# A joint input projection by twenty block products instead of twenty-two

## The chip, the core and the metric

The kernel runs on one core of a Trainium2 chip. A core has five engines that work side by side, each on its own list of instructions, in order: TensorE (PE in the profile, with its weight loads as PEld), VectorE (DVE), ScalarE (ACT), GpSimd (POOL) and SyncE (SP), which here only issues DMAs. They wait for each other through semaphores. TensorE writes to PSUM, a small accumulator memory; VectorE and ScalarE read results out of it. The metric is the time of one execution in microseconds (us) on the device.

## The reference

The program computes two blocks in a row. The first is a linear attention (RWKV-6) with a per-channel decay, for 4 batches, 8 heads, 768 tokens and a head dimension of 48:

```
for t in range(S):
    cur = outer(u * k[t], v[t])
    y[t] = r[t] @ (state + cur)
    state = w[t][:, None] * state + outer(k[t], v[t])
```

Its output, rearranged to 3072 tokens of 384 channels, is x of the second block, a feed-forward layer with 2048 hidden channels:

```
h = x @ w_in                                  # 384 -> 2048
sp = max(h, 0) + log1p(exp(-abs(h)))          # softplus
g = h * erf(sp)
out = g @ w_out                               # 2048 -> 384
```

Everything is in float32.

## The kernel before

The 3072 tokens are worked through in twelve units (`n_steps`, n in the text; the last two are n−2 and n−1) of 256 tokens (128 tokens of two batches). For each unit the attention makes `xT`: three tiles of 128 channels by 256 tokens, channels on the partitions. The feed-forward of a unit follows one to three steps later and is spread in small pieces between the attention's instructions of later units, so that TensorE always has something to do. There is no automatic scheduler: the order is written out by hand (`tc.manual_schedule`), and every engine gets its instructions in the order in which the Python code issues them. `run_late` reads a string of letters and issues one piece for each. The letters that matter here:

- `P` and `Q`: a piece of the output projection (`project_fast`, L1245), of the unit three or two steps back. It is eight matmuls, one of seven block products by which a unit's output is made (a 2x2x2 scheme with seven products in place of eight). Its sums lie in two PSUM tiles `m`, of a pool with two buffers. DVE adds the last products to `o` (L1265, L1270), and SP sends `o` out.
- `S`: `blend`, four DVE instructions (L1222 to L1228) that make the left factors of the seven products from the unit's hidden values, once all of these are there.
- `J`: a piece of the joint input projection (`hidden_of_two`), `T`: its preparation (`join_tokens`), `w`: one instruction of `join_weights`.
- `u`, `v`, `z` (`activate_pair`): softplus of one 128x512 chunk of hidden values on ACT, erf of it on ACT, and the product with the hidden values on DVE. ACT loads a table whenever it changes between softplus and erf.

The input projection of most units (`hidden`, L1123) takes 48 matmuls a unit: 16 groups of 128 hidden channels by three groups of 128 input channels. For the last two units, which come when no attention is left to interleave with, it is done jointly. Two units' tokens, the two halves of the hidden channels (`NG` = 2, eight groups each) and the input channels make a block product, which `hidden_of_two` computes by a scheme with 22 block products for 24. It runs over four pairs of channel groups; in each pair it makes seven pieces `J`, 22 matmuls of 128x256 in all. The sums lie in PSUM in three places: `m0` in the tile `y` and `low` and `high` in the two `pp` tiles; each of the three takes half of both banks of its tile. ACT or DVE reads every finished sum into the hidden values h11, h12, h21, h22 (L1342 to L1365), and a chunk that is complete goes to the list `chunks`, from which `u` takes it.

The weight sums for the joint projection (L1297) and the token differences (L1310) are made by DVE before it starts. In the last attention step (`LATE[n_steps - 1]`) and the lines behind the loop over the steps (at the end of the kernel function) their places among the other pieces are written out.

[...]

Of the kernel before, what the change touches and what calls it, by code (L numbers as in the profile page):

```python
# [11 lines left out]
FP32 = mybir.dt.float32  # L12
# [40 lines left out]
def rights(ap, half):  # L53

    names = "abcdefg"[: len(ap.shape) - 1]
    spread = " ".join(names)
    return ap.rearrange(f"{spread} (n two h) -> {spread} n two h", two=2, h=half)[
        (slice(None),) * len(names) + (slice(None), 1)
    ]


@with_exitstack
def kernel(
# [1004 lines left out]
    later, chunks, started = [], [], []  # L1068
# [136 lines left out]
    def blend(of, *parts):  # L1205

        if of not in blends:
            if of < n_steps - 2:
                tiles = [room[:, n] for n in (1, 2, 3)]
            elif of == n_steps - 1:  # L1210
                tiles = [half_room("words", [P, 2, DM, 2])[:, : FG * C] for _ in range(3)]
            else:
                two = att.tile([P, 2, JP, C], FP32, name="rk1", bufs=1)
                one = ins.tile([P, JP, C], FP32, name="w")
                tiles = [x.rearrange("p n t -> p (n t)") for x in (two[:, 0], two[:, 1], one[:])]
            s1, s2, s4 = (x.rearrange("p (f t) -> p f t", t=C) for x in tiles)
            blends[of] = s1, s2, quarter(of, "21"), s4
        s1, s2, s3, s4 = blends[of]
        a = {what: quarter(of, what) if what not in lanes else lanes[what] for what in ("11", "12", "22")}
        for part in parts or (1, 2, 4, 3):  # L1220
            if part == 1:
                nc.vector.tensor_add(s1, s3, a["22"])  # L1222
            elif part == 2:
                nc.vector.tensor_sub(s2, s1, a["11"])
            elif part == 3:
                nc.vector.tensor_sub(s3, a["11"], s3)
            else:
                nc.vector.tensor_sub(s4, a["12"], s2)  # L1228
# [52 lines left out]
    def third(g, kk):  # L1281

        return w_in_sb[:, g * FG : (g + 1) * FG, kk * P : (kk + 1) * P]

    def join_weights():

        s1, s2, s4 = (
            half_room("words", [P, 2, DM, 2])[:, : FG * P].rearrange("p (f m) -> p f m", m=P)
            for _ in range(3)
        )  # L1290
        a11, a12, a21, a22 = (third(g, kk) for g in range(NG) for kk in range(2))
        turns["joint weights"] = s1, s2, a21, s4
        for out_, a, op, b in (
            (s1, a21, ALU.add, a22), (s2, s1, ALU.subtract, a11),
            (s4, a12, ALU.subtract, s2), (a21, a11, ALU.subtract, a21),
        ):
            nc.vector.tensor_tensor(out=out_, in0=a, in1=b, op=op)  # L1297
            yield

    def join_tokens():  # L1300

        made = ins.tile([P, 2, JP, C], FP32, name="in")
        made = made[:].rearrange("p x n t -> p (x n t)").rearrange("p (i t) -> p i t", t=UNIT)
        t1, t2, t3, t4, less = (made[:, i] for i in range(5))
        one, two = ([xTs[of][:, kk, :] for kk in range(KT)] for of in (n_steps - 2, n_steps - 1))
        for out_, a, b in (
            (t1, two[0], one[0]), (t2, two[1], t1), (t4, one[1], t2), (less, one[2], two[2]),
            (t3, two[1], two[0]),
        ):
            nc.vector.tensor_sub(out_, a, b)  # L1310
        turns["joint tokens"] = one, two, t1, t2, t3, t4, less

    def hidden_of_two():
# [3 lines left out]
        h12 = room[:, 2:4].rearrange("p i n -> p (i n)").rearrange("p (f t) -> p f t", t=UNIT)  # L1317
        h22 = ins.tile([P, 2, JP, C], FP32, name="in")
        h22 = h22[:].rearrange("p x n t -> p (x n t)").rearrange("p (f t) -> p f t", t=UNIT)
        gated[one].extend((h11, h21))  # L1320
        gated[two].extend((h12, h22))
        m0 = y[:, :, 0].rearrange("p e j t -> p e (j t)")
        low, high = (products([P, NE, 2, UNIT], n)[:, :, 0] for n in range(2))

        s1, s2, s3, s4 = turns["joint weights"]
        x, z, t1, t2, t3, t4, less = turns["joint tokens"]
        a11, a12, up, _, a22, down = (third(g, kk) for g in range(NG) for kk in range(KT))

        def add_up(to, start, *factors):

            for k, (a, b) in enumerate(factors):
                for e in range(NE):
                    nc.tensor.matmul(  # L1333
                        to[:, e], lhsT=a[:, 2 * i + e], rhs=b,
                        start=start and not k, stop=True, skip_group_check=True,
                    )

        pairs = FG // 2
        for i in range(pairs):
            f = slice(2 * i, 2 * i + 2)  # L1340
            add_up(m0, True, (a11, x[0]))
            nc.scalar.copy(h11[:, f], m0)  # L1342
            yield
            add_up(low, True, (a12, x[1]), (up, x[2]))
            nc.vector.tensor_add(h11[:, f], h11[:, f], low)
            chunks.append(h11[:, f])
            yield
            add_up(high, True, (s1, t1))
            nc.scalar.copy(h22[:, f], high)
            yield  # L1350
            add_up(m0, False, (s2, t2))
            nc.vector.tensor_copy(h12[:, f], m0)
            yield
            add_up(low, True, (a22, t4), (down, less))
            nc.scalar.copy(h21[:, f], low)
            yield
            add_up(m0, False, (s3, t3), (down, z[2]))
            nc.vector.tensor_add(h21[:, f], h21[:, f], m0)
            nc.vector.tensor_add(h22[:, f], h22[:, f], m0)
            chunks.append(h21[:, f])  # L1360
            if i < pairs - 2:
                chunks.append(h22[:, f])
            yield
            add_up(high, False, (s4, z[1]), (up, z[2]))
            nc.vector.tensor_add(h12[:, f], h12[:, f], high)  # L1365
            if i < pairs - 2:
                chunks.append(h12[:, f])
            elif i == pairs - 1:
                chunks.extend(h[:, 2 * i - 2 : 2 * i + 2] for h in (h12, h22))
            yield  # L1370
# [3 lines left out]
    def activate_pair(what):  # L1374

        if what == "u":
            h = chunks.pop(0)
# [45 lines left out]
    def in_order(s, k):  # L1423
# [15 lines left out]
            "s P", "m w", "ey P m s P P ep P", "m P P", "", "", ""  # L1439
# [7 lines left out]
    def run_late(s, tokens, following=None):  # L1447

        for what in tokens.split():
# [16 lines left out]
            elif what == "T":  # L1466
                join_tokens()
                turns["joint"] = hidden_of_two()
            elif what == "f":
# [26 lines left out]
    joining = join_weights()  # L1496
# [15 lines left out]
    with tc.manual_schedule(  # L1512
# [81 lines left out]
        run_late(s - 1, "S Q w w w")  # L1594
        from_own(s - 1, ready[s - 1][0], 0)
        through_state(s - 1, xTs[s - 1])
        run_late(s, "P P P P T")
        run_late(s, "J J J J J u J u u J")
        run_late(s, "J u v J J v J z z J v v J z u u u J z")
        run_late(s, "J u v J J v J z z J v v J z u u J z")  # L1600
        run_late(s, "J J u v J J z v J z v J z u v J z P P S s ey")
        run_late(s + 1, "P P m s ep P P m P P P S")
# [97 lines left out]
```

## Time and profile before

Three runs took 576.76, 577.13 and 577.54 us. The profiled execution has a span of 575.4 us from its first to its last instruction; its own time outside the span is not recorded, and the median of the runs lies 1.7 us above the span.

| stretch (us from the start) | length | PE busy | DVE busy | ACT busy | granted TensorE clock |
|---|---|---|---|---|---|
| last attention step up to the joint projection, 439.82 to 492.74 | 52.92 | 52.92 | 29.05 | 27.31 | 1.00 |
| joint projection, 492.74 to 530.72 | 37.98 | 37.98 | 19.05 | 28.08 | 1.00 |
| output projection of the last two units and the end, 530.72 to 575.40 | 44.68 | 41.60 | 16.66 | 13.89 | 1.00 |

How to read it: a row is a stretch of the span, and each number the time in which the engine had an instruction at work. An engine's instructions overlap a little at their ends, so the time from one start to the next is somewhat shorter than the duration of one. A bracket behind an instruction in the timelines, such as [2.83 <-PE y L1333], says that the engine was idle for 2.83 us before it, and which instruction ended that. A float32 matmul leaves two records in the trace, so a count of 4 is two matmuls. The last store to memory is issued at 572.74 and lands at about 574.35.

### The profile page before, as it was taken

The numbers are of one execution on the slowest core, as the hardware profiler recorded it, in microseconds if no ns is written. First come the engines' busy times: TensorE is split into PE (matmuls) and PEld (weight loads), VectorE is DVE, ScalarE is ACT, GpSimd is POOL, SyncE is SP. The second block draws the span as 40 slices with busy tenths as digits, with TensorE's granted clock in tenths as the row PEclk, the third lists the DMA queues.
The fourth block names the chain that finished last, engine by engine and source line by source line (L and its number), as shares of the span: only waits on it lengthen the run. The fifth ranks groups of instructions, "written<-read, shape, count | busy, mean of one in ns | idle before, by whom it ended". The sixth has DMA issues, their size and how long they took to land.

```text
span 575.4 us, 16716 instructions
## 1 busy us (share of the span) xinstructions
PE 568.1 (99%) x7336; PEld 503.9 (88%) x7336; DVE 442.7 (77%) x475; ACT 358.0 (62%) x488; POOL 244.7 (43%) x265
## 2 busy tenths in 40 slices
PE   8999999999999999999999999999999999999997
PEld 6688777678998998998998998998898899988997
DVE  7785887999899998798699699599599527255640
ACT  3668777645458858748747756766766661388700
POOL 4567381632885883393384284185173000000000
PEclk9999999999999999999999999999999999999999
DMA  7595662350435325155145145234232201000000
GB/s 263 192 348 214 240 205 68 161 164 3 147 84 168 109 66 171 21 176 166 18 159 167 32 145 172 40 121 162 39 120 74 48 8 37 1 1 2 27 28 27
DMA packets 54081, 63.24 MB, mean 110 GB/s; under 512 B 35160, under 2 KB 40568, under 8 KB 52984
## 3 DMA queue, kind: packets, MB, share of 16 engines
q1 hardware_dynamic: 53624, 61.98, 34.0%
q8 instruction: 57, 0.93, 0.7%
q10 hardware_dynamic: 384, 0.20, 0.1%
q14 instruction: 16, 0.13, 0.1%
HBM read 52.39 MB, written 8.69 MB: 106 GB/s over the span
## 4 chain that ended last, share of the span: by engine, by line
PE 93%; DVE 4%; ACT 2%; issue 1%; POOL 0%; DVEq 0%; ACTq 0%; POOLq 0%
PE m L1245 34%; PE m L1123 33%; PE pp L641 5%; PE pp L1333 4%; PE m L1155 4%; PE y L1333 2%; PE y L673 2%; PE y L699 2%; PE pp L748 2%; PE m L951 1%; DVE in L334 1%; PE pp L960 1%; PE pp L1033 1%; DVE h L1088 1%; ACT rest L267 0%
## 5 line engine op out<-in xcount | busy, mean ns | idle before, releaser
L1123 PE MATMUL m<-xT,w_in_sb 128*128 128x256 f32 x960 | 215.0, 382 | 0.9 <-ACT h L1132 0.7
L1123 PEld LDWEIGHTS m<-xT,w_in_sb 128*128 128x128 f32 x960 | 179.8, 190 | 26.5 <-ACT h L1132 1.4
L334 DVE TENSOR_TENSOR in<-in,tot_sb 128x1024 f32<-128x1024 f32 (+1 forms) x55 | 80.1, 1457 | 12.7 <-PE pp L641 11.4
L1132 ACT COPY h<-m 128x512 f32<-128x512 f32 x80 | 46.1, 580 | 48.5 <-PE m L1123 48.4
L1245 PE MATMUL m<-mixed,h 128*128 128x192 f32 x320 | 56.7, 331 | 0.0
L1245 PE MATMUL m<-w_out_sb,h 128*128 128x192 f32 x320 | 56.2, 329 | 0.0
L1245 PEld LDWEIGHTS m<-mixed,h 128*128 128x128 f32 x320 | 51.8, 190 | 1.0
L1245 PE MATMUL m<-w_out_sb,room 128*128 128x192 f32 x304 | 52.5, 326 | 0.0
L1245 PEld LDWEIGHTS m<-w_out_sb,h 128*128 128x128 f32 x320 | 52.0, 190 | 0.5
L1245 PEld LDWEIGHTS m<-w_out_sb,room 128*128 128x128 f32 x304 | 49.9, 190 | 0.0
L1083 ACT ACT_TABLE_LOAD x30 | 38.5, 1283 | 10.7 <-DVE h L1088 8.5
L463 POOL TENSOR_TENSOR words<-words,own 128x384 f32<-128x384 f32 x21 | 30.1, 1432 | 22.8 <-DVE words L494 13.0
L504 POOL TENSOR_TENSOR words<-words 128x384 f32<-128x384 f32 x28 | 39.7, 1447 | 0.0
L1079 ACT ACT_TABLE_LOAD x30 | 38.5, 1283 | 1.8 <-issue 1.3
L641 PEld LDWEIGHTS pp<-in 48*48 48x48 f32 (+4 forms) x2368 | 30.1, 120 | 10.8 <-issue 3.5
L456 POOL TENSOR_TENSOR own<-rest 128x384 f32<-128x384 f32 x7 | 9.7, 1379 | 61.0 <-ACT o L1251 61.0
L641 PE MATMUL pp<-in 48*48 48x32 f32 (+4 forms) x2368 | 33.9, 206 | 0.2 <-DVE in L334 0.2
L504 POOL TENSOR_TENSOR rk<-words 128x384 f32<-128x384 f32 x28 | 33.4, 1220 | 0.0
L529 DVE TENSOR_REDUCE sums<-rk 128x16 f32<-128x768 f32 (+2 forms) x31 | 31.6, 1020 | 0.0
L408 POOL TENSOR_TENSOR tot_sb<-tot_sb 128x256 f32<-128x256 f32 (+4 forms) x50 | 28.8, 576 | 3.8
L1079 ACT ACTIVATE room<-h 128x1024 f32<-128x1024 f32 x28 | 29.6, 1057 | 0.3
L1245 PE MATMUL m<-mixed,room 128*128 128x192 f32 x160 | 27.7, 327 | 0.0
(206 smaller groups left out, 981.6 us busy)
## 6 DMA issues: line engine op xcount, KB each, us to landing
in<-in_rkw SPq DMA_DIRECT2D x8, 1024.0 KB, 5.2
words<-in_moe_w_in SPq DMA_DIRECT2D x16, 384.0 KB, 5.4
words<-in_moe_w_out SPq DMA_DIRECT2D x16, 384.0 KB, 5.2
words<-in_rk_rows SPq DMA_DIRECT2D x8, 768.0 KB, 6.1
w<-in_rkw SPq DMA_DIRECT2D x11, 512.0 KB
v<-in_v SPq DMA_DIRECT2D x12, 384.0 KB, 5.6
out<-o SPq DMA_DIRECT2D x23, 192.0 KB, 3.0
in<-in_rkw SPq DMA_DIRECT2D x7, 512.0 KB, 5.6
```

The lines of the kernel that those rows point to most:

```text
L334: nc.vector.tensor_mul(halves, halves, view(tots[level - 1], 0, [[1, n], [2, nb], [0, half]]))
L408: nc.gpsimd.tensor_mul(new, pair[:, :, 0], pair[:, :, 1])
L463: engine.tensor_mul(to, to, of[:, :, None, :].to_broadcast([P, NEAR // 2 // half, half, D]))
L504: engine.tensor_mul(to[:, i], r[:, half:], k[:, part * rows + i, None].to_broadcast([P, half, D]),)
L529: nc.vector.tensor_reduce(out=to, in_=of, axis=mybir.AxisListType.X, op=ALU.add)
L641: nc.tensor.matmul(to, lhsT=rk(1, n)[rows(e), s0 : s0 + m], rhs=right, start=True, stop=True,)
L1079: nc.scalar.activation(sp_room, chunks[0], AF.Softplus)
L1083: nc.scalar.activation(at, sp_room, AF.Erf)
L1123: nc.tensor.matmul(ps[:, ff, :], lhsT=w_in_sb[:, g * FG + f + ff, kk * P : (kk + 1) * P], rhs=xT[:, kk, :], start=kk == 0, stop=kk == KT - 1,)
L1132: nc.scalar.copy(h[:, f : f + FT, :], ps[:])
L1245: nc.tensor.matmul(to, lhsT=a[:, f], rhs=b[:, f], start=start and f == 0, stop=f == FG - 1, skip_group_check=True,)
L1333: nc.tensor.matmul(to[:, e], lhsT=a[:, 2 * i + e], rhs=b, start=start and not k, stop=True, skip_group_check=True,)
```

## The change

The joint input projection uses another scheme: the two units' tokens, three groups of input channels and four groups of four hidden channel groups each are a 2x3 by 3x4 block product, which 20 products make in place of 24. The work is done in two rounds (`i`), each for two of the four channel groups of every quarter. A round has 20 pieces `J` of two matmuls each, 128x256. The 20 products are added up in six running sums ("chains" 0 to 5), each 128x512 floats: 0 and 1 are the two halves of `y`, 2 and 3 the halves of the first `pp` tile, 4 and 5 those of the second. After every product its chain's running sum is read into one or two of the eight hidden chunks (`reads`): by an ACT copy (L1386, or L1388 with the sign changed) where it is the chunk's first, by a DVE add or subtraction (L1390, L1392) where it is not. A round has 8 first reads on ACT and 14 on DVE.

Around it: `join_weights` with four DVE instructions of 128x1024 becomes `shared_weights` with 18 of 128x512 on DVE and one on ACT, all issued in the last attention step (before: one of the four there, three behind it). `join_tokens` with five instructions becomes `shared_tokens` with twelve, two of them in that step. Unit n−2's chunks are activated ahead of unit n−1's (`chunks or after`). Three pieces `P` instead of four stand before the joint projection, and three others of the same unit behind it instead of two; the letters `u`, `v` and `z` are placed anew. Some hidden values and blends lie in other SBUF buffers. The diff, cut to the parts named:

```diff
+WEIGHTS = (
+    ("e", "b21", "+", "b31", ""), ("eb11", "b11", "-", "e", ""), ("eb12", "eb11", "-", "b12", ""),
...
+TOKENS = (
+    ("E", "a13", "-", "a12"), ("S", "a11", "+", "a12"), ("K", "a21", "+", "a23"),
+    ("L", "a11", "-", "K"), ("Q", "a11", "+", "a22"), ("F", "E", "+", "a22"),
+    ("M", "E", "-", "K"), ("H", "a12", "-", "a22"), ("R", "a21", "-", "a11"),
+    ("N", "L", "+", "a13"), ("D", "F", "-", "a23"), ("T", "a21", "+", "a22"),
+)
+PRODUCTS = (
+    (0, "a11", "b12", ("c12",), 1), (1, "a11", "k", ("c14",), 1), (2, "E", "b22", ("c12",), -1),
+    (5, "a13", "b2232", ("c12",), 1), (3, "E", "b3134", ("c11",), 1), (0, "L", "eb12", ("c22",), 1),
+    (1, "Q", "m", ("c24",), 1), (2, "F", "n33", ("c13",), -1), (0, "K", "eb34", ("c24",), 1),
+    (1, "a22", "m22", ("c23",), 1), (2, "D", "b33", ("c23",), -1), (0, "M", "g", ("c21",), 1),
+    (1, "H", "b2333", ("c13",), 1), (4, "R", "eb11", ("c21", "c22"), 1), (0, "N", "e", ("c11",), 1),
+    (2, "a23", "r", ("c22",), -1), (3, "D", "b21", ("c21",), 1), (0, "S", "g24", ("c14",), 1),
+    (5, "R", "b13", ("c23", "c24"), 1), (4, "T", "m24", ("c24",), 1),
+)
+STARTS = {"a11b12", "a11k", "Eb22", "a13b2232", "Eb3134", "Reb11", "Rb13"}
+PARTS = {"c11": 2, "c12": 3, "c13": 2, "c14": 2, "c21": 3, "c22": 3, "c23": 3, "c24": 4}
...
-    def join_weights():
-
-        s1, s2, s4 = (
-            half_room("words", [P, 2, DM, 2])[:, : FG * P].rearrange("p (f m) -> p f m", m=P)
-            for _ in range(3)
-        )
...
-            nc.vector.tensor_tensor(out=out_, in0=a, in1=b, op=op)
+    def shared_weights():
...
+        for name, a, op, b, into in WEIGHTS:
+            to = grid[into] if into in grid else extra.pop(0)
+            if op == "n":
+                nc.scalar.mul(out=to, in_=grid[a], mul=-1.0)
+            else:
+                nc.vector.tensor_tensor(
+                    out=to, in0=grid[a], in1=grid[b],
+                    op=ALU.add if op == "+" else ALU.subtract,
+                )
+            grid[name] = to
             yield
...
     def hidden_of_two():
...
-        m0 = y[:, :, 0].rearrange("p e j t -> p e (j t)")
-        low, high = (products([P, NE, 2, UNIT], n)[:, :, 0] for n in range(2))
...
+        sums_in = [y[:].rearrange("p e q j t -> p e (q j t)")[:, e] for e in range(NE)]
+        sums_in += [
+            products([P, NE, 2 * UNIT], n)[:, e] for n in range(2) for e in range(NE)
+        ]
+        half = FG // 2
+        for i in range(2):
+            left, begun = dict(PARTS), set()
+            for chain, a, b, reads, sign in PRODUCTS:
+                to = sums_in[chain].rearrange("p (f t) -> p f t", t=UNIT)
+                for f in range(FT):
                     nc.tensor.matmul(
-                        to[:, e], lhsT=a[:, 2 * i + e], rhs=b,
-                        start=start and not k, stop=True, skip_group_check=True,
+                        to[:, f], lhsT=turns["weights"][b][:, i * FT + f], rhs=turns["tokens"][a],
+                        start=a + b in STARTS and not f, stop=True, skip_group_check=True,
                     )
...
+                for c in reads:
+                    unit, q = int(c[1]) - 1, int(c[2]) - 1
+                    n = q % 2 * half + i * FT
+                    h = gated[(one, two)[unit]][q // 2][:, n : n + FT]
+                    if c not in begun and sign > 0:
+                        nc.scalar.copy(h, to)
+                    elif c not in begun:
+                        nc.scalar.mul(out=h, in_=to, mul=-1.0)
+                    elif sign > 0:
+                        nc.vector.tensor_add(h, h, to)
+                    else:
+                        nc.vector.tensor_sub(h, h, to)
+                    begun.add(c)
+                    left[c] -= 1
+                    if not left[c]:
+                        (chunks, after)[unit].append(h)
+                yield
...
-            h = chunks.pop(0)
+            h = (chunks or after).pop(0)
...
-            "s P", "m w", "ey P m s P P ep P", "m P P", "", "", ""
+            "s P", "m", "ey P w w w w w w w m s P P ep P w w w w w w w w w w w w", "m P P t t", "", "", ""
...
-        run_late(s - 1, "S Q w w w")
+        run_late(s - 1, "S Q")
         from_own(s - 1, ready[s - 1][0], 0)
         through_state(s - 1, xTs[s - 1])
-        run_late(s, "P P P P T")
-        run_late(s, "J J J J J u J u u J")
-        run_late(s, "J u v J J v J z z J v v J z u u u J z")
-        run_late(s, "J u v J J v J z z J v v J z u u J z")
-        run_late(s, "J J u v J J z v J z v J z u v J z P P S s ey")
-        run_late(s + 1, "P P m s ep P P m P P P S")
+        run_late(s, "P P P T t t t t t t t t t t")
+        run_late(s, "J J J J u J J J J J J J J J J v J J u u u z J u v v J J J J v z J v z J")
+        run_late(s, "J J J z J z J J u J J u J u v J J J z J v J v u z J z u J J u P u v v v")
+        run_late(s, "z z v u P u z S z P u u v v")
+        run_late(s + 1, "P z z v v P z z S P P P P P")
         run_late(s + 2, "P P P P P P P")
```

## The prediction

> **What bounds the kernel now.** I read the page first (busy shares), then the chain of waits in order of time for the end of the span, then ScalarE's and VectorE's timelines for the same stretch, and last the list of waits. The page:
>
> ```profile
> span 575.4 us, 16716 instructions
> PE 568.1 (99%) x7336; PEld 503.9 (88%) x7336; DVE 442.7 (77%) x475; ACT 358.0 (62%) x488; POOL 244.7 (43%) x265
> ```
>
> The chain of waits at the end (start, length, engine, tile, line):
>
> ```profile
> 492.74 0.86 PE y L1333 x4
> 493.60 2.59 PE pp L1333 x12
> ...
> 530.72 39.00 PE m L1245 x240
> 569.72 2.61 PE pp L1245 x16
> 572.34 0.02 issue
> 572.36 0.35 DVE o L1277
> ```
>
> TensorE (PE) carries the end without a hole: the joint projection (L1333) runs from 492.74 to 530.72, the output projection (L1245) up to 572.34. A microsecond that PE works less or waits more there moves the end by one. The 88 joint matmuls (two records each) take 37.98, so 0.432 each; one piece of output projection (16 records) takes 2.6.
>
> Who empties PSUM, ScalarE (ACT) and VectorE (DVE):
>
> ```profile
> 493.64 0.58 ACT L1342 COPY h<-y 128x512 f32<-128x512 f32 x1 [3.15 <-PE y L1333]
> 499.42 1.28 ACT L1382 ACT_TABLE_LOAD   x1
> 500.71 1.25 ACT L1382 ACTIVATE room<-h 128x512 f32<-128x512 f32 x2
> 495.43 0.69 DVE L1345 TENSOR_TENSOR h<-h,pp 128x512 f32<-128x512 f32 x1 [6.41 <-PE pp L1333]
> 500.61 0.69 DVE L1358 TENSOR_TENSOR h<-h,y 128x512 f32<-128x512 f32 x1 [2.83 <-PE y L1333]
> 501.22 0.68 DVE L1359 TENSOR_TENSOR in<-in,y 128x512 f32<-128x512 f32 x1
> ...
> 535.96 0.56 DVE L1270 TENSOR_TENSOR o<-o,m 128x384 f32<-128x384 f32 x1 [1.66 <-PE m L1245]
> 536.43 1.22 DVE L1222 TENSOR_TENSOR rk<-h 128x1024 f32<-128x1024 f32 x1
> ```
>
> A first product ends at 493.60 and ACT starts 0.04 later; the first product on `low` ends at 495.33 (8 records of 0.216 after 493.60), DVE starts 0.10 later. A copy takes 0.58, an add 0.69, and the next add starts 0.61 after it. Both engines idle between; PE never waits for them, because each of the three sums (`m0`, `low`, `high`) lies in another tile than the one before it.
>
> What a wait of PE for an evacuation costs, where it occurs (timeline near 224 us):
>
> ```profile
> 224.13 1.06 ACT L1132 COPY h<-m 128x512 f32<-128x512 f32 x2
> 224.76 0.48 PE L1123 MATMUL m<-xT,w_in_sb 128*128 128x256 f32 x1 [0.35 <-ACT h L1132]
> ```
>
> The first copy ends at 224.13 + 0.58 = 224.71, PE starts 0.05 later, and the first matmul takes 0.48 instead of 0.38 (its weights were not loaded ahead): 0.15 in all. So a full turn PE, ACT, PE is 0.04 + 0.58 + 0.15 = **0.77**, and PE, DVE, PE 0.10 + 0.69 + 0.15 = **0.94**.
>
> **The change, part by part.**
>
> *Fewer products.* 80 matmuls for 88: −8 × 0.432 = **−3.45**.
>
> *Six sums in three tiles.* The new sums 0 and 1 are the halves of `y`, 2 and 3 of the first `pp` tile, 4 and 5 of the second. In the built program, which is no trace, a matmul waits for the evacuation of the product before it whenever both lie in one tile, though in different halves; product 2 (sum 1), for one, waits for ACT's copy of product 1 (sum 0). The first three joint matmuls in its list, with what they wait for in brackets:
>
> ```
> L1377 Matmult y_106<-xT_4456,w_in_sb_102 128x256 [waits DMAHW1_49,DMAHW0_49,Activation_49]
> L1377 Matmult y_106<-xT_4456,w_in_sb_102 128x256
> L1377 Matmult y_106<-xT_4456,w_in_sb_102 128x256 [waits Activation_49]
> ```
>
> Counting PRODUCTS from 1, that hits six pairs in each of the two rounds: 1-2, 6-7, 9-10, 12-13 (`y`), 16-17 and 19-20 (`pp`). At the bare turn: three by ACT (1-2, 6-7, 12-13) 3 × 0.77, two by DVE (9-10, 16-17) 2 × 0.94, and 19-20 with two adds, 0.94 + 0.61 = 1.55; together 5.74 a round, **+11.5** for both.
>
> *Queues ahead of the evacuation.* ACT and DVE take their lists in order.
> - First round, 6-7: the first softplus stands in ACT's list ahead of the copies of products 5 and 6, and waits for the add of product 4. From the end of product 4: add done 0.79, table load (1.28) done 2.11, softplus and copy of 5 (steps of 0.53 and 0.48) put the copy of 6 at 3.12 to 3.70, PE goes on at 3.85; product 6 was done at 1.79. Wait 2.05, so 1.28 over the bare turn.
> - Second round, 16-17: DVE has product 14's two adds, 15's, one multiply and 16's subtraction in a row, 0.10 + 4 × 0.61 + 0.69 + 0.15 = 3.38 after product 14, when PE could go on after 1.79: 1.59, or 0.65 over.
> - Second round, 19-20: two multiplies and 18's add stand before the two adds, 3.99 after product 17 against 1.73: 2.26, or 0.7 over.
> - 3-5 and 14-15 (one product between): 0.92 needed, 0.86 there: 0.06 each, four times.
>
> Together **+2.9**.
>
> *One late release behind the joint.* Three pieces of unit n−3 now stand between the joint and unit n−2. Unit n−2's second piece needs the PSUM tile that DVE's last add for unit n−3 (L1270 now, L1299 then) frees. Before, that add runs at 535.96, ahead of the blends (536.43). Now it stands behind the four blends and a multiply. From the joint's end: add of o at 5.28, one step 0.47, multiply and gap 0.76, three dependent blends of 1.25 to 1.30, one of 1.14, a multiply 0.61, the add 0.55: 12.6; with 0.15 PE starts at 12.8 instead of 4 × 2.6 = 10.4. **+2.3** (0 if DVE gains two microseconds, 4 if it loses two).
>
> *Weights and tokens.* The room for them on DVE in the last attention step:
>
> ```profile
> 463.51 1.22 DVE L1088 TENSOR_TENSOR h<-h,y 128x1024 f32<-128x1024 f32 x1 [2.90 <-ACT y L1083]
> 471.20 0.69 DVE L334 TENSOR_TENSOR in<-in,tot_sb 128x512 f32<-128x512 f32 x1 [6.47 <-PE pp L641]
> ```
>
> DVE makes 18 half-size weight sums (0.61 apart, 0.77 where one reads the last) for four of 1.22, and 12 token sums (0.38) for 5; ACT one more copy. The 18 sums, some 12 us, all lie in this step, where one of 1.22 stood; the idle 2.90 and 6.47 take most of them. The scaling at 471.20 slides 2 to 3 us, the state's add at 477.55 by 0.5; PE first needs them near 481 (state products, L699): 0. Without that slack it would be up to 2.7. Token sums that need the last unit come from 488.26 on, the last by 492.1; product 3's `E` is made near 478, `L` (product 6) by 489: 0. The joint starts at 490.1, since three pieces of output projection precede it, not four; the fourth comes behind. SP's and POOL's lists are unchanged, so no DMA moves except with PE.
>
> *Sum:* −3.45 + 11.5 + 2.9 + 2.3 = **+13.2**, with rounding kept 13.1. Against the profiled span 575.4 that is 588.5; the shown runs' median 577.13 lies 1.7 above the span, so **590.2**. Unknown: the restart, 0.05 with the weights loaded ahead to 0.24 with a whole weight load (0.19) behind it, where the row shows 0.15, gives −1.3 to +1.2 over 13 waits; the queue terms may be 0 or twice as large. Behind a waiting matmul stands all of PE's list, so each wait moves the end by its length.
>
> [...]
>
> **Rivals.**
> - *Not slower.* PE waits only for the same sum, not the same tile. Then product 9 of round one waits 0.4 for the copy of 6 (PE goes on at 3.85 after product 4, and would be there at 4 × 0.863 = 3.45), and the late release stays: −3.45 + 0.4 + 2.3 = −0.8, **576.4**; without the late release 574.1. It decides if the thirteen waits together fall below 3.45, so 0.27 each, against a copy of 0.58 alone. [...] Against it: the waits in the program. Chance 0.05 for both forms.
> - *Bare turns only.* The queue terms and the late release vanish: −3.45 + 11.5 = +8, **585**. Speaks for it that DVE and ACT are under 75% busy in this stretch; against it their order is fixed. 0.12.
> - *ACT becomes the bound.* Ten table loads (12.8), 32 activations (17 to 20) and 16 copies (9) are 40 us in a joint of 49, and the second unit's multiplies wait for the last erf; if a load slips behind one more product in each round, +4: **594**. 0.10.
> - *The clock falls.* The first 12 records (L951) take 5.49 us, 0.46 each against 0.216 later; at that pace the 80 matmuls cost 39 more: about **629**. Against it: from 20 to 28 us PE is busy 7.16 of 8 us at a granted clock of 1.00. [...] 0.02.
>
> **How the numbers follow.** My forecast has 0.71, the rivals 0.29. Range: low 585 takes in bare turns, high 594.5 the ACT case; outside it stay the not-slower case and the clock, some 0.15 with errors I don't see. No difference means within 0.2% (1.2 us), about what a measurement of this kernel can tell. Slower 0.95; the not-slower rival splits into same 0.03 (576.4) and faster 0.02 (574).
>
> **What will show it.** The joint's products should show PE gaps with ACT and DVE named as releaser: 0.7 to 1.0 for most pairs, near 2 at the first round's 7, above 1.4 at the second round's 17 and 20; joint from about 490 to 539 instead of 38 long; then one gap near 552 in the output projection, and nothing else. Joint gaps summing below 3 would make it wrong, as would a granted clock below 1.00, or PE waiting ahead of 490, which would mean that the weight sums were not hidden.

## The result and the profile after

The changed kernel takes 592.67 us (median of four runs, 592.17 to 594.4); the kernel before, measured beside it, 576.98. The ratio is **1.0278** with a 95% interval of 1.0262 to 1.0294: slower by 15.7 us. The forecast was 590.2, so the sign and the mechanism held and 2.5 us were missing. The profiled execution has a span of 590.6 us against 575.4, 15.2 more. Its page:

```profile
span 590.6 us, 16712 instructions
...
PE 568.8 (96%) x7320; PEld 499.4 (85%) x7320; DVE 453.6 (77%) x506; ACT 359.2 (61%) x495; POOL 246.3 (42%) x265
...
PE   8999999999999999999999999999999997787897
```

TensorE was 99% busy before; now slices 34 to 38 of the 40 in its row (14.8 us each) fall to 7 and 8 tenths, and they lie in the joint projection (489.55 to 540.86) and just behind it. The list of waits of TensorE names them (what waited, on what, us in total, times, longest):

```profile
PE y L1377 <- ACT rk L1386: 3.8, 4, 1.8
PE pp L1377 <- DVE in L1390: 3.4, 2, 2.1
PE m L1274 <- DVE o L1299: 2.0, 1, 2.0
PE pp L1377 <- DVE rk L1392: 2.0, 2, 1.2
PE y L1377 <- DVE in L1390: 1.7, 2, 0.9
...
PE y L1377 <- ACT h L1386: 1.4, 2, 0.7
```

Before, no wait of the joint projection or of the output projection was in this list. Now there are twelve waits of L1377 on an engine that reads PSUM, and one of the output projection (L1274) on DVE's last add into `o` (L1299). TensorE's timeline shows where they stand (start, length, operation; the bracket is the idle time ahead of it and what ended it):

```profile
489.55 1.03 PE L1377 MATMUL y<-xT,w_in_sb 128*128 128x256 f32 x4
491.25 1.13 PE L1377 MATMUL y<-xT,w_in_sb 128*128 128x256 f32 x4 [0.68 <-ACT h L1386]
492.21 1.03 PE L1377 MATMUL pp<-in,w_in_sb 128*128 128x256 f32 x4
...
495.06 1.03 PE L1377 MATMUL y<-in,words 128*128 128x256 f32 x4
497.84 1.13 PE L1377 MATMUL y<-in,w_in_sb 128*128 128x256 f32 x4 [1.76 <-ACT rk L1386]
...
510.00 1.13 PE L1377 MATMUL pp<-tot_sb,w_in_sb 128*128 128x256 f32 x4 [0.78 <-DVE rk L1392]
...
539.89 1.13 PE L1377 MATMUL pp<-spread,w_in_sb 128*128 128x256 f32 x4 [2.05 <-DVE in L1390]
540.86 2.76 PE L1274 MATMUL m<-w_out_sb,room 128*128 128x192 f32 x16
...
553.45 2.87 PE L1274 MATMUL m<-mixed,h 128*128 128x192 f32 x16 [2.03 <-DVE o L1299]
```

A product is two matmuls, so four records, and in a continuous run a product follows the last after 0.863. Product 2 starts 1.70 after product 1, because both sums lie in `y`; product 3 follows it after 0.96. ScalarE in the same stretch:

```profile
490.61 0.58 ACT L1386 COPY h<-y 128x512 f32<-128x512 f32 x1 [0.54 <-PE y L1377]
...
494.91 1.28 ACT L1409 ACT_TABLE_LOAD   x1 [1.91 <-DVE h L1390]
496.20 0.63 ACT L1409 ACTIVATE room<-h 128x512 f32<-128x512 f32 x1
496.74 0.57 ACT L1386 COPY h<-pp 128x512 f32<-128x512 f32 x1
497.20 0.59 ACT L1386 COPY rk<-y 128x512 f32<-128x512 f32 x1
```

The first copy ends at 491.19, product 2 starts at 491.25: it waited for that copy, of the other half of its tile. Ahead of product 7 the table load and the first softplus stand in ACT's list, so the copy of product 6 comes at 497.20 only. And VectorE behind the joint projection:

```profile
547.45 1.22 DVE L1251 TENSOR_TENSOR own<-h 128x1024 f32<-128x1024 f32 x1
548.71 1.22 DVE L1253 TENSOR_TENSOR own<-own,h 128x1024 f32<-128x1024 f32 x1
549.97 1.22 DVE L1257 TENSOR_TENSOR w<-h,own 128x1024 f32<-128x1024 f32 x1
551.11 1.22 DVE L1255 TENSOR_TENSOR h<-h 128x1024 f32<-128x1024 f32 x1
552.25 0.68 DVE L1417 TENSOR_TENSOR in<-in,room 128x512 f32<-128x512 f32 x1
552.85 0.55 DVE L1299 TENSOR_TENSOR o<-o,m 128x384 f32<-128x384 f32 x1
```

The add into `o` comes behind the four blends and a multiply, and its end at 553.40 lets the output projection go on at 553.45.

Three lengths are used for all that follows, since the stretch ahead of the joint projection differs by 2 to 4 us between executions of kernels that are alike up to there (the joint projection starts at 489.55 and 491.56, with own tiles at 490.39 and 494.15). *Joint* is the time from the first joint matmul to the first one behind, *tail* from there to the start of TensorE's last record. *Loss* is what the products take over 0.863 each.

| kernel | joint starts | joint | loss | tail | span |
|---|---|---|---|---|---|
| before | 492.57 | 37.99 | 0 | 41.44 | 575.4 |
| after | 489.55 | 51.31 | 16.79 | 46.33 | 590.6 |

The tail grew by 4.89: 2.60 of it is the one piece of output projection that stood ahead of the joint projection before, which therefore starts earlier now; 2.29 is new. So the change cost 13.32 + 2.29 = 15.6 by these stretches, and 0.43 of it is missing from the spans' difference because the stretch ahead was shorter by that in this execution (492.57 − 2.59 would be 489.98).

### The profile page after: what moved, and what is told of

Its sections match the earlier page's. It is cut to its first block, busy times and chain, and to the rows that moved or that the text cites. A ratio compares the mean times of both kernels' runs of the same rounds, so it can differ in the third digit from the quotient of the medians.

```text
span 590.6 us, 16712 instructions
## 1 busy us (share of the span) xinstructions
PE 568.8 (96%) x7320; PEld 499.4 (85%) x7320; DVE 453.6 (77%) x506; ACT 359.2 (61%) x495; POOL 246.3 (42%) x265
## 4 chain that ended last, share of the span: by engine, by line
PE 80%; DVE 10%; issue 3%; POOL 2%; ACT 2%; DMA 2%; SPq 0%; DVEq 0%; POOLq 0%; ACTq 0%
PE m L1274 33%; PE m L1152 28%; PE pp L670 5%; PE y L1377 3%; PE pp L1377 3%; DVE in L363 2%; PE y L702 2%; PE m L1184 2%; PE y L728 2%; PE pp L777 1%; DMA words<-in_moe_w_in 1%; PE pp L989 1%; DVE in L1390 1%; DMA u_sb<-in_u 1%; DVE own L680 1%
## 5 line engine op out<-in xcount | busy, mean ns | idle before, releaser
L363 DVE TENSOR_TENSOR in<-in,tot_sb 128x1024 f32<-128x1024 f32 (+1 forms) x55 | 78.4, 1426 | 5.5 <-PE pp L670 4.1
L1274 PE MATMUL m<-mixed,h 128*128 128x192 f32 x320 | 56.8, 331 | 2.0 <-DVE o L1299 2.0
L1274 PE MATMUL m<-w_out_sb,h 128*128 128x192 f32 x320 | 56.1, 329 | 0.0
L1274 PEld LDWEIGHTS m<-mixed,h 128*128 128x128 f32 x320 | 51.7, 190 | 3.2 <-DVE o L1299 2.3
L1274 PEld LDWEIGHTS m<-w_out_sb,h 128*128 128x128 f32 x320 | 52.0, 190 | 0.5
L1274 PE MATMUL m<-w_out_sb,room 128*128 128x192 f32 x288 | 49.7, 326 | 0.0
L1274 PEld LDWEIGHTS m<-w_out_sb,room 128*128 128x128 f32 x288 | 47.3, 190 | 0.1
L318 POOL TENSOR_TENSOR w_out_sb<-w_out_sb,rest 128x768 int32<-128x768 int32 x8 | 18.0, 2254 | 21.4 <-DVE w_out_sb L310 21.3
```

The lines of the kernel that those rows point to most:

```text
L363: nc.vector.tensor_mul(halves, halves, view(tots[level - 1], 0, [[1, n], [2, nb], [0, half]]))
L1274: nc.tensor.matmul(to, lhsT=a[:, f], rhs=b[:, f], start=start and f == 0, stop=f == FG - 1, skip_group_check=True,)
```

## The experiments

The theory: a joint matmul waits for the read-out of the product before it whenever both running sums lie in one tile, and the late add into `o` costs one more wait. The rivals: it isn't the tiles but ACT or DVE that are too slow in all; the weight sums on DVE delay the start; the order of the activations makes most of the waits.

**The same work, neighbours in other tiles.** The running sums are dealt out anew, so that chains 0 and 1, 2 and 3, 4 and 5 no longer share a tile:

```diff
+        sums_in = [sums_in[n] for n in (0, 2, 4, 3, 5, 1)]
         half = FG // 2
```

> The changed kernel with the six running sums dealt out otherwise over the same three tiles (0 and 5 in y, 1 and 3 in the first pp tile, 2 and 4 in the second), so that only one pair of products a round (18-19) lies in one tile, not six. Theory (PE waits because two successive products share a tile): the direct turns of 0.94 to 1.05 fall from twelve to two; what is left are 18-19 (1.2 and 1.4) and five pairs with one product between, 0.2 to 0.8 each, the first softplus ahead of product 7 (1.6), and the 2.0 at the late release. Together 9 to 9.5 of waits, less 3.45 for fewer products: about +6 against the kernel before, 583. Rival (ACT and DVE are too slow for 22 reads a round, wherever the sums lie): no change from the changed kernel, 592.7.

Measured: 583.6 us (583.26 to 584.02) against 576.92, ratio 1.0114 [1.0099, 1.013]; joint 41.84, loss 7.32, tail 46.34. What is left of the waits in the joint projection:

```profile
PE y L1378 <- DVE h L1391: 2.0, 2, 1.1
...
PE pp L1378 <- DVE rk L1391: 1.5, 2, 0.9
PE pp L1378 <- ACT h L1387: 1.3, 1, 1.3
...
PE y L1378 <- DVE in L1391: 0.5, 1, 0.5
```

One line that only says which half of which tile a sum takes gives back 9.5 of the joint's 13.3 us. Number, kind and order of all instructions on every engine are the same, so neither ACT's nor DVE's amount of work makes those 9.5. Six waits remain, where sums that still share a tile follow each other closely.

**Each sum in its own tile.** Six tiles of 128x512 floats. The pools of `y` and `pp` are closed ahead of the joint projection, and a new pool takes their place:

```diff
+    early = ctx.enter_context(ExitStack())
+    ps_p = early.enter_context(tc.tile_pool(name="ps_p", bufs=1, space=PSUM))
+    ps_y = early.enter_context(tc.tile_pool(name="ps_y", bufs=1, space=PSUM))
...
-        sums_in = [y[:].rearrange("p e q j t -> p e (q j t)")[:, e] for e in range(NE)]
-        sums_in += [
-            products([P, NE, 2 * UNIT], n)[:, e] for n in range(2) for e in range(NE)
-        ]
+        early.close()
+        ps_j = ctx.enter_context(tc.tile_pool(name="ps_j", bufs=1, space=PSUM))
+        sums_in = [ps_j.tile([P, 2 * UNIT], FP32, name=f"j{n}")[:] for n in range(6)]
```

> The changed kernel with a tile of its own for each of the six sums: y and the two pp tiles are given up before the joint projection and six tiles of 128x512 take their place; order, engines and sizes are unchanged. Theory: PE waits for the same sum alone, so all gaps in the joint projection vanish (at most 0.4 behind the first softplus) and it takes 34.5; the late release (2.0 to 2.5) stays: 577.0 - 3.45 + 2.4 = about 576. Rival (readers too slow): the joint stays near 51 and the time near 592.

Measured: 576.95 us (ten runs, 574.77 to 578.54) against 576.92, ratio 0.9997 [0.998, 1.0014]; joint 34.63, loss 0.1 (one product that ran 0.1 late), tail 46.33. Its timeline of TensorE:

```profile
490.39 1.89 PE L1378 MATMUL j<-xT,w_in_sb 128*128 128x256 f32 x8
492.12 1.03 PE L1378 MATMUL j<-in,w_in_sb 128*128 128x256 f32 x4
...
524.16 1.03 PE L1378 MATMUL j<-spread,w_in_sb 128*128 128x256 f32 x4
525.02 2.76 PE L1275 MATMUL m<-w_out_sb,room 128*128 128x192 f32 x16
...
537.61 2.87 PE L1275 MATMUL m<-mixed,h 128*128 128x192 f32 x16 [2.03 <-DVE o L1300]
```

Products 1 and 2 are now one run of eight records, and not one bracket is left up to 525.02. All 16.7 us of waits in the joint projection came from the sharing of tiles; 80 matmuls in 34.63 are 0.433 each, as before. The wait of product 7 behind the table load, 1.92 in the changed kernel, is gone, since product 7 no longer needs the copy that stands behind that load. The wait on `o` stayed, to the hundredth.

**The late add into `o`.** The piece that waits for it is put ahead of the blends:

```diff
-        run_late(s, "z z v u P u z S z P u u v v")
+        run_late(s, "z z v u P u z P z S u u v v")
```

> The changed kernel with unit n-3's last output piece and its DVE add ahead of the four blends of unit n-2, where they were behind (P z S for S z P); PE's order is the same. Theory: the wait of 2.03 before unit n-2's second piece goes and nothing takes its place, since the blends are needed two pieces later: -2.0 to -2.5 against the changed kernel, about 590.5; the joint projection stays at 51.3. Rival: the blends, now some 1.5 later, make PE wait at the third or fourth piece instead: 592 to 593.

Measured: 593.3 us (588.73, 593.12, 593.48, 594.36) against 576.92, ratio 1.0267 [1.0225, 1.0309]. In the profile the wait is gone and the tail is 44.04, so 2.29 shorter, exactly the new part of it; but the runs' median did not fall. Beside the changed kernel, on one chip:

> The changed kernel itself, beside the others of this call on one chip. Expected: 592 to 593 against 577 before, joint projection 51.3 long, 2.0 at the late release.

> The kernel of e3_release again, beside the changed kernel: there its profiled execution lost the wait of 2.03 (joint end to the last matmul 44.04 for 46.33), but its timed runs did not get shorter (593.3). Theory: they differ by chance, and here it is 2.3 below the changed kernel, 590.3. Rival: runs without the profiler have another wait, and it stays at or above the changed kernel, 593.

Measured: the changed kernel 593.49 us (591.52 to 593.81), ratio 1.0271 [1.0231, 1.031]; with the add early 591.31 us (six runs, 589.43 to 593.32), ratio 1.0244 [1.0214, 1.0274]. The difference is 2.2 us, about the wait; but the two intervals overlap, and the first four runs stood 0.6 above the 592.67 of the changed kernel. That the wait costs 2.29 in the profile is shown; that the runs give it back is likely. The profiles of these two runs show something else as well, which the section on the clock tells.

**Both together.**

```diff
+    early = ctx.enter_context(ExitStack())
...
+        sums_in = [ps_j.tile([P, 2 * UNIT], FP32, name=f"j{n}")[:] for n in range(6)]
...
-        run_late(s, "z z v u P u z S z P u u v v")
+        run_late(s, "z z v u P u z P z S u u v v")
```

> The two together: six tiles, and the add ahead of the blends. Theory: no wait of PE is left behind the last attention step, and only the eight matmuls fewer count: 577.0 - 3.45 = 573.5. Rival: with PE ahead by 17 us ACT's activations (40 us of work behind the joint's start) come too late for unit n-2 or n-1, and a wait of 2 or more takes back most of it: 576 or above.

Measured: 574.05 us (ten runs, 572.66 to 578.0) against 576.92, ratio **0.9951 [0.9936, 0.9965]**: 0.5% below the kernel before. Joint 34.63, tail 44.04, so the joint is 3.36 shorter than before and the tail, without the piece that changed sides, as long as before: the saving of eight matmuls, whole. In these stretches the two faults were all that the change lost.

**The kernel before, made to wait.** The old scheme with `low` and `high` moved into the two halves of one `pp` tile (the start flag is then set by the first matmul into that tile alone):

```diff
-        low, high = (products([P, NE, 2, UNIT], n)[:, :, 0] for n in range(2))
+        low, high = (products([P, 2, NE, UNIT], 0)[:, n] for n in range(2))
...
-                        start=start and not k, stop=True, skip_group_check=True,
+                        start=start and not k and (to is m0 or not e), stop=True, skip_group_check=True,
```

> The kernel before with its 22 products, and only the places of two sums changed: low and high lie in the two halves of the first pp tile, a bank each, instead of one in each pp tile. The second pp tile stays unused in the joint projection. Theory (the shared tile alone costs it, not the new scheme): the four direct pairs low-high wait 1.05 each, and sums with one product between meet waits of 0.07 to 1.2; joint projection 42 to 44.6 for 38.0, so 581 to 583.6. Rival (the new scheme's reads, weight or token sums cost it): 577.

Measured: 584.33 us (582.47 to 585.85) against 576.32, ratio 1.0122 [1.0085, 1.0159]; joint 44.88, loss 6.90, tail 41.44.

```profile
PE pp L1333 <- DVE h L1345: 3.4, 4, 0.9
...
PE pp L1333 <- ACT in L1349: 1.1, 1, 1.1
```

The old 22 products, which showed no wait, lose 6.9 us in the joint projection when two of their three sums share a tile. Four equal turns through DVE cost 1.01 + 0.10 each, about 1.1. So it isn't the twenty-product scheme as such. The joint came out 0.3 and the time 0.7 above the upper ends of what was expected. In its profile the rest of the longer span, 1.8, lies ahead of the joint projection; it comes up again below.

**The softplus ahead of product 7.** The first `u` two products later:

```diff
-        run_late(s, "J J J J u J J J J J J J J J J v J J u u u z J u v v J J J J v z J v z J")
+        run_late(s, "J J J J J J u J J J J J J J J v J J u u u z J u v v J J J J v z J v z J")
```

> The changed kernel with the first softplus two products later in ACT's list (behind the copies of products 5 and 6). Theory: the wait before product 7 falls from 1.76 to the bare 0.68, but products 7 to 9 now meet the table load and the activation, which take back 0.5: joint projection 50.6 to 50.8 for 51.3, about 592.1. Rival (the wait has nothing to do with the load): joint unchanged, 592.7.

Measured: 593.62 us (591.59 to 595.06) against 576.32, ratio 1.0282 [1.0246, 1.0318]; joint 50.83, tail 46.34. TensorE:

```profile
498.77 1.13 PE L1377 MATMUL y<-in,w_in_sb 128*128 128x256 f32 x4 [0.68 <-ACT rk L1386]
499.74 1.03 PE L1377 MATMUL pp<-in,words 128*128 128x256 f32 x4
501.19 1.13 PE L1377 MATMUL y<-in,words 128*128 128x256 f32 x4 [0.42 <-ACT in L1386]
```

The wait ahead of product 7 fell from 1.76 to 0.68, the bare turn, and the table load now holds back the copy of product 7, which product 9 needs: 0.42. Of 1.08 saved, 0.6 came back in products 7 to 9, so the joint is 0.48 shorter. In the runs this can't be seen (593.49 for the changed kernel beside it). Only one softplus was moved here; but with the order of the activations as it was, other tiles took 9.5 us out of the joint and own tiles all of the waits, so the rival that the order makes most of them falls.

**Ten of the weight sums left out.**

```diff
-            else:
+            elif into not in grid:
                 nc.vector.tensor_tensor(
```

> Left out: the ten VectorE weight sums that are written in place of an old weight; the eight into new tiles and the ScalarE negation stay, so ten of the left factors are unsummed weights. Theory (the weight sums lie in VectorE's idle time of the last attention step): ten instructions of about 0.6 us less change nothing; no wait of TensorE goes, the joint projection stays 51.3 long with the same waits (1.9 before product 7, 2.0 before product 20 of round two), the tail behind it 46.3, and the stretch before it as in the changed kernel, so 592 to 593.5 (ratio 1.026 to 1.030). Rival (the sums delay the scaling of the state, and with it TensorE, by up to 2.7): the scaling of the state moves ahead and the joint starts up to 2.7 earlier, time 590 to 590.5, with the joint's length unchanged.

Measured: 592.88 us (591.94 to 595.26) against 576.77, ratio 1.0281 [1.0238, 1.0325]; joint start 489.08, joint 51.38, tail 47.95. The tail is 1.6 longer than expected, because this profile has one of the falls of the clock that are told below. DVE's scaling of the state in the changed kernel:

```profile
472.19 0.69 DVE L363 TENSOR_TENSOR in<-in,tot_sb 128x512 f32<-128x512 f32 x1
```

and with ten sums less:

```profile
470.31 0.69 DVE L363 TENSOR_TENSOR in<-in,tot_sb 128x512 f32<-128x512 f32 x1 [5.26 <-PE pp L670]
```

The scaling runs 1.9 earlier, and the time does not change. These ten of the eighteen sums on DVE are hidden; the other eight and the token sums were left out in no run.

## A clock that falls, and why

Some profiles of the changed kernel showed what the first did not: the granted clock at half for a few us behind the longest wait. The re-run of the changed kernel, in stretches (from:to, length, TensorE's busy time and records, granted clock, DMA share, GB/s):

```profile
537.59:541.00 3.41, 1.36 (x7) 1.00 0.00 0
541.00:544.41 3.41, 3.41 (x13) 0.50 0.00 0
```

The wait of 2.05 at 539.64 leaves TensorE busy 1.36 of 3.41 us, and for exactly the next 3.41 us the clock is 0.50. The tail of that profile is 48.02, 1.69 more than in the first. Of six profiles of kernels with this longest wait, three show such a fall, each 3.41 long. To see whether it follows from the waits, three of them were made longer, by two operations of DVE each that cancel:

```diff
                     else:
                         nc.vector.tensor_sub(h, h, to)
+                    if a + b == "a23r" or (c == "c24" and a + b == "Rb13" and not i):
+                        nc.vector.tensor_add(h, h, to)
+                        nc.vector.tensor_sub(h, h, to)
```

> The read-outs of product 16 (both rounds) and of product 19 (first round) are followed by one more add and one more subtraction of the same sum into the same chunk, which cancel; nothing is left out. Each of the three waits behind them grows by two steps of VectorE, 1.2 us: from 0.94, 1.54 and 1.36 to about 2.2, 2.8 and 2.6 (loss of a product against 0.863), product 20's of round two stays 2.2; the joint grows from 51.3 to about 55.0 where the clock stays. Theory (the clock is set anew every 3.41 us on a fixed grid by how busy TensorE was in the 3.41 us before; seen so far: half clock after 0.32 to 0.37, full after 0.42 and more): each of the four waits that leaves TensorE busy for less than 0.4 of one stretch of the grid is followed by exactly one stretch of 3.41 us at 0.50, which costs 1.7 us each; with waits of 2.2 to 2.8, between one and three of the four. [...]

> The kernel of the run before once more, for another position of the grid. Theory: again one stretch of 3.41 us at 0.50 behind each wait that leaves TensorE busy for less than 0.4 of one stretch of the grid, and none behind the others; which waits these are differs from the run before, and all falls lie a whole number of 3.41 us apart. Rival: none, or falls at the same places as before whatever the grid.

Measured: 600.05 and 601.93 us (one run each), joint 59.82 and 59.96; that is the 55.0 expected at a full clock and about three times 1.7 for the falls. The first shows three falls (from 511.52, 518.34 and 542.24), the second four (from 511.49, 518.32, 542.21 and 562.69), all 3.41 long and, within one profile, whole multiples of 3.413 apart: 2, 7 and 6 stretches in the second. Its stretches on that grid:

```profile
508.08:511.49 3.41, 1.19 (x6) 1.00 0.00 0
511.49:514.90 3.41, 3.41 (x10) 0.50 0.02 7
514.90:518.32 3.42, 0.60 (x3) 1.00 0.00 0
518.32:521.73 3.41, 3.27 (x8) 0.50 0.00 0
538.80:542.21 3.41, 0.77 (x4) 1.00 0.00 0
542.21:545.62 3.41, 3.41 (x10) 0.50 0.00 0
559.28:562.69 3.41, 1.38 (x9) 1.00 0.14 52
562.69:566.10 3.41, 3.41 (x13) 0.50 0.02 5
```

In the first of the two runs the wait on `o` fell a little otherwise onto the grid:

```profile
559.30:562.71 3.41, 1.58 (x10) 1.00 0.16 58
562.71:566.12 3.41, 3.41 (x23) 1.00 0.00 0
```

TensorE was busy for 1.19, 0.60, 0.77 and 1.38 of 3.41 us ahead of the four falls, and for 1.58 where none came. In the first profile of the changed kernel the clock's record in the trace runs from 5.53 to 592.62, which is 172 whole stretches; on that grid the longest wait leaves TensorE busy for 1.53 of the stretch from 538.01, and no fall follows. So among these large matmuls the bound lies between 1.38 and 1.53, some 0.40 to 0.45 of a stretch. No wait of the second run is above 2.82 in its timeline, and in the re-run the wait ahead of the fall was 2.05. The expectation's shares of 0.32 to 0.37 and 0.42 are smaller than those of the rows, because they count a matmul as the time to the next start (0.216 or 0.163) and not by its record, which is longer; by that count the four stretches ahead of the falls are at most 0.37 full, those with 1.53 and 1.58 are 0.42 and 0.43, and the bound of 0.4 held. That the grid would lie elsewhere in the second run did not come true: the first fall came 0.03 earlier, so this run can't tell a grid from fixed places in the kernel. The other profiles can: the same wait of 2.05 was followed by a fall in three of six. And across the seven profiles with falls in them the first one comes at 158.50, 158.05, 158.30, 149.86, 149.85, 7.17 and 5.89 stretches from the span's start, so the grid does not begin with the kernel.

Two earlier oddities have a part of their answer here. The profile of the version with both mends shows the clock at 0.50 from 24.46 to 31.29, and that of the old scheme with shared tiles from 20.12 to 23.53, long before the joint projection; their joint projections began at 494.15 and 494.35. TensorE's records fill 1.70 and 2.04 of the 3.41 us ahead of those falls, more than the bound above, and the second of the two stretches at 0.50 follows one that is 2.88 full. These are small matmuls of 64x48 and the like; for them the bound does not hold, and no run shows what takes its place. Each of the stretches with 1.70 and 2.04 also holds idle time of TensorE for which the profile names no releaser, 2.04 us ahead of 25.00 and 1.38 us ahead of 20.13; of the other lists of TensorE's waits, those of the re-run and of the version with the softplus two products later have such lines too, with waits of 0.4 to 0.7. So the half clock need not have made the whole of the late start; what caused the idle time, and how much each of the two made, stays open.

## Why the prediction was right, and what was mis-sized

| term | forecast | measured | from |
|---|---|---|---|
| eight matmuls fewer | −3.45 | −3.36 | joint 34.63 (own tiles) against 37.99 |
| waits in the joint, with their queues | +14.4 | +16.7 | joint 51.31 against 34.63 (own tiles) |
| late add into `o` | +2.3 | +2.29 | tail 46.33 against 44.04 |
| weights and tokens | 0 | 0 | ten sums left out: no change |
| sum | +13.1 (+13.2 from the terms as printed) | +15.6 | runs: +15.7 |

*Six sums in three tiles* was right in every pair that it named, and the runs show it from three sides: a loss of 7.3 with neighbours spread, of 0.1 with own tiles, and of 6.9 in the old scheme with a shared tile. The mis-sized term is **the bare turn**, forecast at 0.77 through ACT and 0.94 through DVE. By pair, as loss over 0.863 each, with the 0.10 of the product behind the wait:

| pair | forecast | measured |
|---|---|---|
| 1-2 and 12-13 in both rounds, 6-7 in the second (ACT) | 0.77 | 0.94 |
| 9-10, both rounds (DVE) | 0.94 | 1.12 |
| 16-17, first round (DVE) | 0.94 | 1.05 |
| 19-20, first round (two adds) | 1.55 | 1.65 |
| 6-7, first round (table load) | 2.05 | 2.02 |
| 16-17, second round (queue) | 1.59 | 1.46 |
| 19-20, second round (queue) | 2.26 | 2.32 |
| 3-5 and 13-15, both rounds (one product between) | 0.06 | 0.26 |

The last row's second pair stands in the prediction as 14-15; the sums that share a tile are those of 13 and 15.

In the turn by ACT the step that failed is "ACT starts 0.04 later". The 0.04 was counted from 493.60, the end of a piece in the chain of waits, whose start (492.74) lies 0.17 behind that of the first joint matmul's record (492.57). Counted from the starts, the time at which the next product could begin is 489.55 + 0.863 = 490.41, and ACT's copy begins at 490.61: 0.20, not 0.04. A record lasts 0.38 while the next follows after 0.216, so 0.16 of each matmul lies under the next one. From the end of product 1's last record (490.57) it is 0.04 again: what the sum left out is this 0.16, since it set the turn against products counted from start to start. In a run of matmuls the 0.16 is free; at a bare turn it is paid (0.94 for 0.77). (The profile models the ends of matmuls, so the split into 0.16 and 0.04 is less sure than the 0.20, which goes by starts.) The 0.10 of the turn by DVE was counted from record ends in the same way; by starts it is 0.28 ahead of product 10 (500.89 against 500.61) and 0.20 ahead of product 17. The copy of 0.58 and the restart of 0.05 and 0.10 were right. Product 2's first record took 0.320 to the next start instead of 0.216, which is that 0.10, also as forecast.

Adding up the rows: the five bare turns by ACT were 0.9 short, the three by DVE 0.5, 19-20 of the first round 0.1, the four pairs with one product between 0.8; four times a product ran 0.08 late at its second record (products 9 and 12 of each round), 0.3, for which no run shows a reason. The three pairs with a long queue were forecast 0.1 too high in all: the queue, not the turn, ends those waits, and the 0.16 passes while DVE or ACT is still at other work. Together 2.4 to 2.5, the whole of what was missing.

*Queues ahead of the evacuation* held: 2.02 for the table load (2.05), and later `u` moved it as its place in ACT's list says. *One late release* held: 2.3 forecast, 2.29 measured. *Weights and tokens* at nothing held: the joint projection began at 489.55 (forecast 490.1), and TensorE is busy for all of the 52.75 us ahead of that.

The rivals. *Not slower* needed that PE waits only for the same sum; the first brackets refute it. The version with own tiles is the one that behaves so: there TensorE writes one sum while ACT and DVE read others, and the joint takes 34.63, with a loss of 0.1. The wait was the program's, which goes by tiles; whether TensorE could write one half of a tile while the other is read was not shown. *Bare turns only* falls by the queue rows. *ACT becomes the bound* falls: with own tiles its list is the same, it is busy for 39.79 of the 52.00 us from 489 to 541, and in the joint, up to 525.02, PE never waits for it. *The clock falls* was wrong as put, for all 80 matmuls at half pace; in small it does occur, one stretch of 3.41 us and some 1.7 us in three of six profiles, and it wasn't in the sum.

## What to carry to other kernels

Before running sums are packed into halves of a PSUM tile, look in the built program which matmuls then wait for a reader: a sum's own half may have been read long ago while its tile is not free, and a tile for each sum cost nothing here (the products took 34.63 us, a loss of 0.1) and was worth 16.7 us. Price a turn TensorE, reader, TensorE from the start of one matmul to the start of the next in a run, not from the ends that the records give: 0.20 to 0.28, the reader's own time, and 0.15 here. Where a wait replaces a wait, ask which instruction then stands first in the reader's list, and which of the kernel's own orders put it there.

## What the hardware showed that was not expected

- TensorE's granted clock fell to 0.50 for 3.41 us at a time, and in the second run with longer waits the falls began 2, 7 and 6 times 3.413 us apart. Among large matmuls these falls followed how full the stretch before was: half clock behind 1.38 us of busy time and less, full behind 1.53 and more. Small matmuls did not keep to this bound: there falls came behind 1.70, 2.04 and 2.88. So a wait of 2.05 was followed by a fall, and a tail 1.69 longer, in the re-run and by none in the first profile; that this makes part of the 2 us by which runs of these kernels scatter is likely, but was only argued.
- By its record, the end of a float32 matmul of 128x256 lies 0.16 behind the moment at which the next could start (a record of 0.38, the next start after 0.216). It appears in no list of waits; in the time it came back at the bare turns, by ACT 0.94 for 0.77.
- ACT's first softplus begins 0.01 after its table load of 1.28 (494.91 and 496.20): nothing more is paid for a change of table here.
